# Half batch 4 of the attention turned by the DMA crossbar instead of by TensorE, with smaller masks and a new order of steps

## The chip, the cores and the metric

The kernel runs on one core of one Trainium2 chip. The metric is the device time in microseconds (us). Executions over 1.5% slower than the fastest of the same kernel are left out of the means. A ratio is the mean time of one kernel's fast runs over that of the other's of the same rounds, so it is not quite the ratio of the medians that stand beside it. Brackets give its 95% interval.

## The reference

Windowed attention on 8 batches, 8 heads, 576 tokens, 64 dimensions, and then a two-layer feed-forward over all 4608 tokens:

```python
rel = pos[:, None] - pos[None, :]
mask_plain = (rel >= 0) & (rel < 32)                              # heads 0 to 3
mask_dil = (rel >= 0) & (rel < 32 * 4) & (rel % 4 == 0)           # heads 4 to 7
scores = np.where(masks, q @ k.T / sqrt(64), -1e9)
attn = exp(scores - max) / sum                                    # over the keys
x = (attn @ v) rearranged to (4608 tokens, 512)
h = x @ w_in                                                      # 512 -> 2048
out = np.maximum(0.01 * h, h) @ w_out                             # 2048 -> 512
```

## The kernel before

The kernel is a list of steps, given as one string and issued in that order; each engine works off its own share in order. PE is TensorE, DVE VectorE, ACT ScalarE, POOL GpSimd and SP SyncE. A half batch n is four heads of one batch (even n the plain heads, odd n the dilated ones), and it has three units of attention. The steps that the argument needs:

- `gq:n` and `lq:n` load q and k of a half batch, `gq` as f16 through POOL's (software) queue, `lq` as f32 on SP's queue. `lq:n:b:P` waits until POOL reaches it. `lv` loads v and `lw` the weights, both on POOL's queue.
- `cq`, `cv` cast or copy on V (DVE), P (POOL) or A (ACT).
- `B:n:pair:..` turns q and k on PE (2 x 18 transposes a call); `T:n` turns them by the DMA crossbar, the transpose that the DMA engines do on the way.
- `S`, `M`, `D` are scores, mask, values of a unit. `S:u:b` adds the mask as a bias by two matmuls on PE, `S:u:m` leaves it to `M` on DVE. `D:u:l` divides by a logarithm and an exponential on ACT, `D:u:r` by DVE's reciprocal.
- `I:c:j` and `O:t:g` are the two layers of the feed-forward.
- `Z:n` is n matmuls of zeros into a PSUM tile that nobody reads. They keep PE busy while data is still on its way; they are called warmers here.

```python
PROGRAM = """
Z:12 gq:3:b lq:1:1 lq:1:0 Z:1 cq:1:k:V:1 lv:1:b lq:0:0 lq:0:1 Z:2 bias cq:1:q:A:1 B:1:1:AA Z:2
... (some 600 steps more) ...
"""
NPE = 5                      # half batches below this are turned on PE

        elif f == "Z":
            wp = psa.tile([128, 512], FP32, tag="den", name="wp")      # one buffer
            for _ in range(int(a[0])):
                nc.tensor.matmul(wp, warm[:, 0:128], warm, start=True, stop=True)

    def transpose(n):                                                  # T:n
        ...
                nc.sync.dma_start_transpose(t.rearrange("p (c r) -> p c r", r=96), qkh[n, nm][0:96, 0:1536])

    def pe_transpose(n, p, nm, eng):                                   # B:n:p
        ...
                nc.tensor.transpose(tp[r, 64 * t:64 * t + 64], h[r, t, :], ident[r, r])

    def load_qk(n, pairs, gate=None):                                  # lq
        ...
            if gate is not None and nm == "q":
                gate.memset(t[0:1, 0, 0:1], 0.0)       # the load waits for this engine

    def ff_out(t, g, queue):
        if g == 0:
            ops[t] = psm.tile([128, 512], FP32, tag="pm", name="op")
        op = ops[t]
        ...
        for c0, c1 in ((0, 256), (256, 512)) if last else ((0, 512),):
            for j in range(0 if last else 4 * g, 4 * g + 4):
                nc.tensor.matmul(op[:, c0:c1], gt[:, j, g0:g0 + 128], w2[j // 4][:, j % 4, c0:c1], ...)
            if g == 3:
                nc.scalar.copy(out=ob[:, c0:c1], in_=op[:, c0:c1])
                queue.dma_start(out[128 * t:128 * t + 128, c0:c1], ob[:, c0:c1])
```

The softmax here doesn't subtract the row's maximum and nothing guards it: scores larger than these inputs give would overflow.

## Time and profile before

| | before |
|---|---|
| time | 322.21 us, 2 runs, 321.96 to 322.46; the profiled run took 321.16 |
| span of the profile | 319.5 us |
| PE busy | 98%, full clock in every slice |
| first feed-forward group starts | 26.51 us |
| last matmul starts | 315.93 us |

The profiled run is 1 us faster than the median of the same kernel. In the eleven runs of this kernel beside the first batch of experiments the times went from 321.17 to 323.33, so a difference of 1 us between two single traces says little.

PE's list of waits tells what is to be won at most: it lists for each line of the kernel what PE stood for, as total us, number of times, longest. L418 is the warmers, L359 the first layer and L374 the second.

```profile
PE wp L418 <- DVE xT L113: 1.3, 1, 1.3
PE hp L359 <- ACT gt L361: 1.0, 2, 0.6
PE op L374 <- ACT ob L378: 0.5, 1, 0.5
```

After the first warmer (which waits for its zeros) the waits come to about 2 us in all. A change can therefore take little more than what it takes from PE's own work.

The first feed-forward group, in the timeline of PE (start, duration, line, operation; a bracket at the end of such a line gives the idle time before it and what ended it):

```profile
26.51 1.49 PE L359 MATMUL hp<-xT,w 128*128 128x384 f16 x8
```

This is the view of PE's weight loads, one of which goes ahead of each matmul; the first column is its start, the second its duration:

```profile
3.45 0.15 PEld L418 LDWEIGHTS <-xT 128*128 128x128 f16 x1 [0.28 <-issue]
3.88 0.15 PEld L418 LDWEIGHTS <-xT 128*128 128x128 f16 x1 [0.28 <-issue]
4.31 0.99 PEld L418 LDWEIGHTS <-xT 128*128 128x128 f16 x5 [0.28 <-issue]
```

Inside a block the warmers follow each other every 0.43 us at first (3.45, 3.88, 4.31) and then every 0.215 us (five in 0.99): PE's clock starts at half, and the trace's record of the granted clock has the full one from 4.35 us on.

### The profile page before, as it was taken

How to read it: one execution, taken by the hardware profiler on the slowest of the kernel's cores; microseconds unless marked ns; L12 is line 12 of the kernel's file. 1: busy time of each engine (PE TensorE's matmuls, PEld its weight loads, DVE VectorE, ACT ScalarE, POOL GpSimd, SP SyncE). 2: the span in 40 equal slices, each digit the busy share in tenths (PEclk: the TensorE clock that was granted, in tenths of full speed). 3: DMA queues.
4: the chain of work that ended last, by engine and by line, in shares of the span. 5: the costliest groups of instructions: out<-in, count | busy, mean ns of one | idle time of the engine just before them, and what ended most of it. 6: DMA issues, size and time to landing. Idle time of an engine off the chain costs nothing.

```text
span 319.5 us, 6740 instructions
## 1 busy us (share of the span) xinstructions
PE 312.5 (98%) x2821; PEld 184.5 (58%) x2821; DVE 125.5 (39%) x196; ACT 190.8 (60%) x375; POOL 75.5 (24%) x113
## 2 busy tenths in 40 slices
PE   8999999999999999999999999999999999999995
PEld 3556765566655655665556556555665555655544
DVE  3586435354475675572521860423224340300000
ACT  3378872768666655767557926764774764453421
POOL 8683400253234043330041500430000000000001
PEclk9999999999999999999999999999999999999999
DMA  7999999999999829999399387391000000000102
GB/s 202 249 206 208 211 170 188 229 184 195 119 238 206 200 55 161 287 159 224 65 230 130 72 207 155 49 168 65 1 35 33 35 35 34 33 35 33 66 35 99
DMA packets 89902, 42.38 MB, mean 133 GB/s; under 512 B 69776, under 2 KB 85136, under 8 KB 89872
## 3 DMA queue, kind: packets, MB, share of 16 engines
q1 hardware_dynamic: 58080, 21.83, 34.7%
q0 software_dynamic: 29344, 15.93, 33.7%
q10 hardware_dynamic: 2448, 4.20, 3.6%
q8 instruction: 22, 0.36, 0.5%
q14 instruction: 8, 0.07, 0.1%
HBM read 36.70 MB, written 9.44 MB: 144 GB/s over the span
## 4 chain that ended last, share of the span: by engine, by line
PE 90%; ACT 4%; DMA 3%; issue 1%; POOL 0%; DVE 0%; ACTq 0%; POOLq 0%
PE hp L359 39%; PE op L374 38%; PE sps L286 4%; PE den L312 3%; DMA kh<-in_k_dram 3%; PE o L320 2%; ACT ln L325 1%; PE tp L233 1%; ACT rec L326 1%; PE wp L418 1%; ACT er L289 1%; PE sps L270 0%; ACT ob L378 0%; ACT gt L361 0%; POOL qh L169 0%
## 5 line engine op out<-in xcount | busy, mean ns | idle before, releaser
L359 PE MATMUL hp<-xT,w 128*128 128x384 f16 (+1 forms) x832 | 140.7, 314 | 1.3 <-ACT gt L361 1.0
L374 PE MATMUL op<-w,gt 128*128 128x512 f16 (+1 forms) x592 | 138.9, 374 | 0.5 <-ACT ob L378 0.5
L361 ACT ACTIVATE gt<-hp 128x384 f16<-128x384 f32 (+1 forms) x208 | 94.5, 465 | 65.9 <-PE hp L359 64.9
L359 PEld LDWEIGHTS <-w 128*128 128x128 f16 x832 | 89.6, 114 | 45.7 <-issue 2.5
L374 PEld LDWEIGHTS <-gt 128*128 128x128 f16 x592 | 56.0, 98 | 54.4 <-issue 0.6
L337 DVE TENSOR_TENSOR xT<-o,rec 128x384 f16<-128x384 f32 (+1 forms) x64 | 34.0, 554 | 81.0 <-ACT rec L326 75.9
L379 POOL DMA_DIRECT2D out_dram<-ob x20 | 11.3, 564 | 180.3 <-ACT ob L378 178.7
L328 DVE RECIPROCAL rec<-den 128x384 f32<-128x384 f32 x14 | 35.8, 2555 | 44.3 <-PE den L312 44.3
L289 ACT ACTIVATE er<-sps 128x768 f16<-128x768 f32 (+1 forms) x48 | 38.6, 804 | 20.8 <-PE sps L286 20.7
L378 ACT COPY ob<-op 128x512 f32<-128x512 f32 (+1 forms) x37 | 21.2, 573 | 28.3 <-PE op L374 28.2
L296 DVE TENSOR_TENSOR em<-er,mask 128x768 f16<-128x768 f16 (+1 forms) x43 | 26.8, 645 | 10.2 <-ACT er L289 10.0
L286 PE MATMUL sps<-qT,kT 64*128 64x96 f16 (+1 forms) x448 | 19.0, 209 | 0.1
L325 ACT ACTIVATE ln<-den 128x384 f32<-128x384 f32 x34 | 16.4, 483 | 3.8 <-PE den L312 3.3
L326 ACT ACTIVATE rec<-ln 128x384 f32<-128x384 f32 x34 | 17.8, 524 | 1.1
L286 PEld LDWEIGHTS <-kT 64*128 64x128 f16 (+1 forms) x448 | 12.1, 106 | 10.0 <-issue 7.1
L320 PEld LDWEIGHTS <-vh 128*64 128x64 f16 (+1 forms) x448 | 15.4, 110 | 2.4
L320 PE MATMUL o<-em,vh 128*64 128x96 f16 (+1 forms) x400 | 15.0, 201 | 0.0
L312 PE MATMUL den<-em,ones 128*64 128x384 f16 (+1 forms) x86 | 15.0, 345 | 0.0
L192 POOL CAST kh<-kf 96x512 f16<-96x512 f32 (+1 forms) x12 | 7.0, 627 | 31.7 <-DMA kf<-in_k_dram 31.7
L418 PE MATMUL wp<-xT 128*128 128x512 f16 x35 | 11.7, 431 | 1.7 <-DVE xT L113 1.3
L177 POOL DMA_DIRECT2D vh<-in_v_dram x8 | 10.7, 1339 | 5.1 <-PE hp L359 2.3
L182 POOL DMA_DIRECT2D vh<-in_v_dram x16 | 10.1, 637 | 2.5 <-PE o L320 2.2
(58 smaller groups left out, 114.3 us busy)
## 6 DMA issues: line engine op xcount, KB each, us to landing
out_dram<-ob POOLq DMA_DIRECT2D x20, 256.0 KB, 2.3
out_dram<-ob ACTq DMA_DIRECT2D x15, 256.0 KB, 2.0
qf<-in_q_dram SPq DMA_DIRECT2D x5, 576.0 KB, 7.0
kf<-in_k_dram SPq DMA_DIRECT2D x5, 576.0 KB, 7.8
vh<-in_v_dram POOLq DMA_DIRECT2D x8, 288.0 KB, 7.6
qf<-in_q_dram SPq DMA_DIRECT2D x6, 384.0 KB, 6.6
kf<-in_k_dram SPq DMA_DIRECT2D x6, 384.0 KB, 8.1
w<-in_moe_w_in_dram POOLq DMA_DIRECT2D x4, 512.0 KB, 12.0
```

The costliest lines, as they stand in the source:

```text
L286: nc.tensor.matmul(sps[0:kp, hh, w * x:w * x + w], ka, qa, start=not pe_mask, stop=not pe_mask or x == len(tiles) - 1)
L289: nc.scalar.activation(out=er[0:kp], in_=sps[0:kp, :, 0:384], func=AF.Exp, scale=SCALE)
L296: nc.vector.tensor_tensor(out=em[0:kp].rearrange("p h (t c) -> p h t c", c=w), in0=er[0:kp].rearrange("p h (t c) -> p h t c", c=w), in1=ba ...
L312: nc.tensor.matmul(den[64 * hh:64 * hh + 64, 0:384], ones[0:kp], em[0:kp, hh, :], start=True, stop=True)
L320: nc.tensor.matmul(o[64 * hh:64 * hh + 64, w * x:w * x + w], vt[0:kp, sl, :], em[0:kp, hh, w * x:w * x + w], start=True, stop=True)
L326: nc.scalar.activation(out=rec, in_=ln, func=AF.Exp, scale=-1.0)
L328: nc.vector.reciprocal(out=rec, in_=den[:, 0:384])
L337: nc.vector.tensor_tensor(out=out_x, in0=ins[0], in1=ins[1], op=ALU.mult)
L359: nc.tensor.matmul(hp[:, 0:w], w1[j // 4][:, i, j % 4::4], xT[:, i, x0:x0 + w], start=(i == 0), stop=(i == 3))
L361: nc.scalar.activation(out=gt[:, j, g0:g0 + w], in_=hp[:, 0:w], func=AF.Prelu, alpha=0.01)
L374: nc.tensor.matmul(op[:, c0:c1], gt[:, j, g0:g0 + 128], w2[j // 4][:, j % 4, c0:c1], start=(j == 0), stop=(j == 15))
L378: nc.scalar.copy(out=ob[:, c0:c1], in_=op[:, c0:c1])
```

## The change

The intent: PE is the bound, so two of its ten transpose calls go to the DMA crossbar; the last output tile gets a second PSUM tile so that its second half need not wait for a copy; the masks are built from 96 columns instead of 384 on POOL; and the whole order is redone.

```diff
-Z:12 gq:3:b lq:1:1 lq:1:0 Z:1 cq:1:k:V:1 lv:1:b lq:0:0 lq:0:1 Z:2 bias cq:1:q:A:1 B:1:1:AA Z:2
-cq:1:q:P:0 Z:4 lv:0:b Z:1 cq:1:k:V:0 Z:1 S:4:b gq:2:b B:1:0:AV ...
+Z:2 gq:3:b lq:1:1 lq:1:0 Z:1 lv:1:b lq:0:0 lq:0:1 Z:1 cq:1:q:P:1 bias Z:3 gq:2:b Z:1 lv:0:b lw:0:0
+mask Z:2 cq:1:k:V:1 Z:1 cq:1:q:A:0 Z:9 B:1:1:VA cq:1:k:V:0 Z:7 lw:0:1 lw:0:2 Z:2 S:4:b B:1:0:AV ...
+... lw:1:1 I:0:1 D:2:lp lq:4:b:P I:0:2 I:0:3 M:11 lq:5:b:P ... cv:3:P:b I:0:13 I:0:14 cq:4:k:P:b
+D:9:rp I:0:15 I:1:0 Z:2 D:11:r ... cq:4:q:P:b I:1:4 O:0:0 B:2:0:AA I:1:5 M:10 lv:2:b lv:4:b lv:5:b
+... cq:5:q:A:b O:2:0 cv:2:P:b ... T:5 T:4 lq:6:b ... Z:1 M:8 D:7:lp ...
@@
-    NPE = 5
+    NPE = 4
@@ masks
-    def band(t, one, other):         # POOL: two memsets, two selects, 384 columns, for bias and for mask
+    def band_bias():                 # POOL: two selects of 96 columns; DVE copies them three times
+    def band_mask():
+        nc.vector.tensor_scalar(out=mask, in0=bias, scalar1=-1.0, scalar2=None, op0=ALU.is_ge)
@@ ff_out
         for c0, c1 in ((0, 256), (256, 512)) if last else ((0, 512),):
+            if c0:
+                op = psm.tile([128, 512], FP32, tag="pm", name="op")
```

(The program string is cut; the memset of `ident` also moves from POOL to DVE.) The first 15 warmers of before stand in three blocks ahead of the first transposes (12, 1 and 2).

## The prediction

> **What bounds the kernel now.** I read the page first (busy times, then the slices), then the chain of waits in order of time, then the timelines of the first 50 us and the last 15, and last the DMA queues stretch by stretch.
>
> ```profile
> PE 312.5 (98%) x2821; PEld 184.5 (58%) x2821; DVE 125.5 (39%) x196; ACT 190.8 (60%) x375; POOL 75.5 (24%) x113
> PEclk9999999999999999999999999999999999999999
> PE 90%; ACT 4%; DMA 3%; issue 1%; POOL 0%; DVE 0%; ACTq 0%; POOLq 0%
> ```
>
> PE is busy for 98% of the span, at full clock, and is 90% of the chain that ended last; no other engine passes 60%. The matmul ends are modelled, so I check it by rate. In the chain in order of time, groups that run without a wait read like this:
>
> ```profile
> 184.01 1.30 PE hp L359 x8
> 185.31 1.73 PE op L374 x8
> 314.30 1.92 PE op L374 x16
> ```
>
> That is 162 ns for a 384-wide matmul of the first layer, 216 ns for a 512-wide one of the second, 120 ns for the 256-wide ones of the end; a run of twelve 192-wide ones takes 0.99 us, 82 ns each. So the feed-forward alone is 704 x 0.162 + 128 x 0.082 + 560 x 0.216 + 32 x 0.120 = 114.0 + 10.5 + 121.0 + 3.8 = 249 us of PE. Attention (48 score steps at 0.28 to 0.46, 48 value steps at 0.45) adds some 36 us, the PE transposes 10 x 0.69 = 7, the warming matmuls about 9. Sum 301 of 319.5. What is left is start, end, some waits in the first 30 us, and about 0.1 us at each of some tens of changes of work. Once the feed-forward has begun, PE hardly waits: the chain leaves PE for a few us at three places only (56 to 60, 174 to 179, 253 to 256 us), mostly overlapped; lost there is 0.4 to 0.7 us each.
>
> Two edges matter. The lead-in: the first feed-forward group starts at 26.5 us, a second burst at 28.6. And the end:
>
> ```profile
> 313.88 0.37 ACT L378 COPY ob<-op 128x256 f32<-128x256 f32 x1 [1.16 <-PE op L374]
> 314.28 0.34 ACTq L379 DMA_DIRECT2D out_dram<-ob  x1
> 314.30 1.91 PE L374 MATMUL op<-w,gt 128*128 128x256 f16 x16 [0.46 <-ACT ob L378]
> ```
>
> Here PE stands 0.46 us because both halves of the last token tile share one PSUM tile, and the second waits for the copy of the first.
>
> The third thing to see is the DMA. The slices show it 99% busy up to about 100 us. In the stretch 33 to 38 us its queues read:
>
> ```profile
> q0 software_dynamic: 268, 0.98, 96.7%
> q1 hardware_dynamic: 266, 0.07, 10.0%
> ```
>
> Equal packets, but the weights (software queue) move 3.7 KB in each and the half batch load on the other queue 256 B. A half batch of the even kind, loaded while weights flow, crawls. The load of half batch 6, issued at 29.5 us, landed 17.5 (q) and 26.5 us (k) later.
>
> **What the Trainium skill says.** "VectorE: DVE Perf Modes", The three transpose paths: 390 ns for a 128x128 transpose on TensorE, 1309 ns by the DMA crossbar. In this trace 36 transposes of 64x64 keep PE for 0.69 us, and one crossbar instruction holds its queue 1.2 to 4 us and lands after 5 to 6: slower, but not on PE. The trade is only good because PE is the bound. "TensorE: Matmul & The Clock Gate", Back-to-back issue gap: N/2.4 + 2.5 ns, 216 for N = 512; the trace has 216. So no order makes the feed-forward cheaper. "DMA: Bandwidth & Descriptors", Issuing engines are not separate DMA queues: all queues share the 16 engines and interleave; the equal packets above agree.
>
> **The change part by part.**
> 1. Half batch 4 leaves PE: two calls, 72 transposes, 2 x 0.69 = 1.4 us off PE, all in the stretch where PE is the bound (67 to 71 us). Gone too are three ACT copies (0.64 each) and one on DVE (0.75), which do not bound. In their place come an f32 load, two casts on POOL of 1.6 us each and two crossbar transposes on SP.
> 2. End: a PSUM tile of its own for the last half, -0.46 us.
> 3. Biased scores: 7 instead of 5 steps are masked on PE, two matmuls of 384 columns each (0.33 us a step). One is in the lead-in (counted in 5), one later: +0.33 us. Two mask multiplications (0.64) leave DVE.
> 4. Division by logarithm in 37 steps instead of 34: DVE loses 3 x 2.55 us, ACT gains 3 x 1.0. Neither is the bound.
> 5. Masks and lead-in. POOL loses two 384-wide memsets and four 384-wide selects of 0.5 to 0.6 us (now two of 96 columns), some 2.5 us; DVE gains about 0.6. But POOL's early work is feeding DMA queues that have a backlog until 43 us, so this does not bring data 2.5 us sooner. The fixed points stay: k of half batch 3 lands at 12.1 us and the software queue delivers in its order. I walked the new order by hand from 12.5 us, when the transposes of 3:0 are done, with the durations of this trace. The last cast for 0:1 (POOL, after data at 14.8) is ready at 16.2; 0:1 turned to 16.9; value step 3 to 17.4, seven warmers to 18.9, step 4 to 19.4, scores 0 to 20.1, three warmers, transposes 3:1 to 21.4, scores 1 to 22.1, transposes 2:1 to 23.2, step 1 to 23.7, scores 11 to 24.4, steps 0 and 5 to 25.8, scores 2 to 26.5. ACT, which takes more of the copies now, is full from 19.4 and gives step 0 its reciprocal at 26.5, so the product is there at 27.3 and the first feed-forward group starts then. Five groups, value step 2 and scores 9 are done at 31.4. The old kernel has these at 32.0 and besides them scores 7 and 10 and the transposes 2:0 (0.3 + 0.3 + 0.69 = 1.3 us). So the new lead-in is 31.4 + 1.3 - 32.0 = 0.7 us behind. There are 50 warming matmuls for 35; the 12 more before the first group (12 x 0.215 = 2.6 us) fill time that would be waited.
> Sum of what is sure: -1.4 - 0.46 + 0.33 + 0.7 = -0.8 us.
> 6. The DMA order. Loads of half batches 4 and 5 are now issued behind the second-layer weights' first two requests. The old trace fits a rule of eight software transfers in flight (the ninth stands until the first lands), so POOL reaches the gate of these loads at about 20.5 us, not 29.5. They contend with weights. I estimate their landing from the old trace: there q of half batch 5 landed at 58.9, behind all that the new one has ahead of it plus the v of 2, 5 and the q, k of 4, which used about 8.3 us of the DMA between 42 and 57. So q of 5 lands at about 50.6, k of 4 a little before. ACT, which now casts q of 5 itself, is reached at about 49. POOL casts 4 to about 52, issues v of 2 behind that, and it lands 7.6 us (median row) after 51.9, at 59.5; the copy of 1.5 us makes 61, while PE wants it at about 58. This may cost 0 to 4 us; whoever wrote the order placed one warmer just there, so a short wait was seen. I take +0.6.
>
> **The rivals.**
> A. PE work falls and nothing else happens: -1.4 - 0.46 + 0.33 is -1.5, and if the lead-in gains from earlier requests (weights asked for at 8 to 13 us instead of 13 to 16) 1 to 2 us more: 318.5 to 320.5. For it: PE's 90% of the chain. Against: the DMA backlog.
> B. A load wait takes the place of the PE work: ACT stands on q of 5 and PE on v of 2 at 48 to 62 us: 324 to 328. For it: 256 B packets crawl behind weights, and POOL stood 23.0 us on k of half batch 5 in the old trace, with v requests now behind such a wait. Against: the old order met its landings nearly exactly, so the new one was likely fitted with care.
> C. ACT becomes the bound in the lead-in, through copies moved from DVE: +1 to +2 us, 322 to 324. Over the whole it has 40% to spare.
>
> **Range and chances.** Before is 322.2. -0.8 + 0.6, and some weight on A because such an order is usually kept when it helps, gives 321.4. Eight in ten: 317.5 to 326. To be 2% faster (under 315.8) PE would have to lose 6.4 us; removed work, end and all found waits together hardly reach that: 4%. To be 2% slower (over 328.7) needs B in full: 5%. Within 2%: 91%.
>
> **What would show it.** PE rows: the transposes at 288 instead of 360, the bias matmul at 14, warmers 50. The last half starting without a wait on ACT. First feed-forward group at 27 to 28 us; if at 24 or 25, my lead-in is wrong and A is right. Feed-forward rates unchanged at 162 and 216 ns. Around 48 to 62 us: PE busy throughout speaks for A; an idle PE released by DVE or ACT, behind POOL's copy of v 2 or the cast of q 5, speaks for B. Two more crossbar rows than 34. Wrong altogether if the clock falls, or if transposes in the DMA hold back later loads so that score steps after 90 us wait.

## The result, and the profile after

325.79 us (two runs, 325.23 and 326.35) against 322.21: ratio 1.0111 [1.0075, 1.0146]. The time is within 2% of before and inside the predicted range, if only by 0.2 us. But the prediction's own estimate lay 0.8 us below the old kernel, and the time came out 3.6 us above.

The page of after: busy times, then the chain that ended last by engine and by line.

```profile
PE 317.0 (98%) x2768; PEld 184.0 (57%) x2768; DVE 105.6 (33%) x172; ACT 201.7 (62%) x396; POOL 76.6 (24%) x112
...
PE 85%; DMA 11%; POOL 1%; ACT 1%; issue 1%; DVE 1%; POOLq 0%
PE op L382 35%; PE hp L365 35%; DMA kf<-in_k_dram 8%; PE wp L426 4%; PE sps L292 4%; PE den L318 3%; DMA vh<-in_v_dram 2%; PE o L326 2%; PE tp L239 1%; PE sps L276 1%; POOL qh L207 0%; POOL vh L216 0%; ACT rec L332 0%; POOL kh L207 0%; DVE xT L343 0%
```

Two things stand out. PE issues 53 matmuls fewer (2768 for 2821: 72 transposes gone, 15 warmers and 4 bias matmuls more), and yet it is *busier*, 317.0 for 312.5 us. And the chain now goes over DMA for 11% of the span; the load of k alone (`kf`) is 8%. The list of PE's waits (L326 is the product with v):

```profile
PE wp L426 <- DVE xT L119: 1.4, 1, 1.4
PE o L326 <- POOL vh L216: 1.3, 1, 1.3
PE hp L365 <- DVE xT L343: 0.4, 1, 0.4
```

The waits on ACT are gone, one on POOL's copy of v has come. The waits after the first warmer are hardly longer than before (2.2 us for 1.9), so most of the 5 us of span stands in the trace as busy time of PE, not as waits.

Where in time? The first feed-forward group starts 3.1 us later, in the timeline of PE:

```profile
29.57 1.46 PE L365 MATMUL hp<-xT,w 128*128 128x384 f16 x8 [0.44 <-DVE xT L343]
```

and the last matmul starts at 320.98 for 315.93, 5.05 us later. I added up PE's start-to-start times (from the start of one matmul to the start of the next), split at the start of the 21st matmul of the first layer, where five groups are done:

| part | us | how |
|---|---|---|
| lead-in, to that matmul | +3.2 | 33.95 - 31.98, and 1.25 of attention work (scores 7 and 10, transposes 2:0) that after has still to do there |
| 72 transposes off PE | -1.37 | their start-to-start time |
| last output tile | -0.62 | the wait of 0.46 and the restart behind it |
| bias matmuls | +0.42 | one more biased score step after this point |
| wait for v of half batch 2 | +1.5 | 1.67 start-to-start, where 0.19 is usual |
| three late warmers (`Z:2`, `Z:1`) | +1.0 | their time and the restarts around them (but see e10) |
| rest | +0.9 | not itemized; PE changes its kind of work 309 times for 296 in this part |
| sum | +5.0 | |

Since before's trace is 1 us faster than its median and after's 0.6 slower, some 1.6 of the 5.0 is chance between two runs; the medians differ by 3.6.

**The lead-in.** The warmers in it take 14.48 us of PE's start-to-start time for 11.20 before: +3.28, about as much as the lead-in lost. Part of that is number, part is how they are cut up. The view of the weight loads, after:

```profile
2.50 0.10 PEld L426 LDWEIGHTS <-xT 128*128 128x128 f16 x1 [0.54 <-issue]
3.14 0.10 PEld L426 LDWEIGHTS <-xT 128*128 128x128 f16 x1 [0.54 <-issue]
3.78 0.10 PEld L426 LDWEIGHTS <-xT 128*128 128x128 f16 x1 [0.54 <-issue]
...
7.14 1.61 PEld L426 LDWEIGHTS <-xT 128*128 128x128 f16 x8 [0.34 <-issue]
```

The first three stand at the head of new blocks and come 0.64 us apart, not 0.43: a new block is a new tile in the one buffer, and its first matmul comes only about when the last one of the block before has ended (the trace gives a warmer 379 ns in the median and 634 at most, so the spacing of 0.64 is one whole matmul, where inside a block the next one follows into the one under way). It costs 0.21 us a block here. The full clock was granted at 6.24 us for 4.35. At full clock a new block costs as much (0.43 us start to start for 0.215). The row of warmers before the first transposes tells the sum (start, duration, count), before:

```profile
1.35 5.31 PE L418 MATMUL wp<-xT 128*128 128x512 f16 x15 [1.35 <-DVE xT L113]
```

and after:

```profile
1.41 7.84 PE L426 MATMUL wp<-xT 128*128 128x512 f16 x20 [1.41 <-DVE xT L119]
```

**The load of half batches 4, 5 and v 2.** In the chain of waits in order of time (start, duration, what):

```profile
22.05 27.07 DMA kf<-in_k_dram
...
49.24 0.06 POOL kh L207
...
50.02 0.82 POOL kh L207
50.84 1.50 POOL qh L207 x2
52.33 7.75 DMA vh<-in_v_dram
...
60.13 1.41 POOL vh L216
```

k of half batch 4 is asked for at 22.05 and has landed after 27 us; only then does POOL cast it, cast q, issue v of half batch 2, wait 7.75 us for it, and copy it. PE came to this product at about 60.1 and ran it at 61.59:

```profile
61.59 0.36 PE L326 MATMUL o<-em,vh 128*64 128x96 f16 x8 [1.31 <-POOL vh L216]
```

Why 27 us: the DMA queues of after in the stretch 35 to 40 us (packets, MB, share of an engine):

```profile
q0 software_dynamic: 272, 0.97, 95.9%
q1 hardware_dynamic: 271, 0.07, 10.1%
```

The two queues move as many packets as each other, but the weights put 3.6 KB in one (0.97 MB over 272) and the half batch 256 B (0.07 MB over 271). The Trainium skill, "DMA: Bandwidth & Descriptors", Queues, rings and completion order, says that each engine goes round between its queue rows at packet granularity; this trace agrees, 272 to 271 (what the trace counts as a packet, of 256 B or 4 KB, may be smaller than the page's). A load in small packets gets a small share of the bytes (here 0.07 MB of 1.04) for as long as a queue of large packets is full.

**The end** is as planned. Before had a gap of 0.46 us between the two halves of the last tile; after the second-layer matmuls run in one row of 59 to the end, the change of tile within it:

```profile
311.76 9.48 PE L382 MATMUL op<-w,gt 128*128 128x512 f16 x59
```

### The profile page after: what moved, and what is told of

It reads as the page before. It is cut to its first block, busy times and chain, and to the rows that moved or that the text cites. A ratio compares the mean times of both kernels' runs of the same rounds, so it can differ in the third digit from the quotient of the medians.

```text
span 324.6 us, 6650 instructions
## 1 busy us (share of the span) xinstructions
PE 317.0 (98%) x2768; PEld 184.0 (57%) x2768; DVE 105.6 (33%) x172; ACT 201.7 (62%) x396; POOL 76.6 (24%) x112
## 3 DMA queue, kind: packets, MB, share of 16 engines
HBM read 36.70 MB, written 9.44 MB: 142 GB/s over the span
## 4 chain that ended last, share of the span: by engine, by line
PE 85%; DMA 11%; POOL 1%; ACT 1%; issue 1%; DVE 1%; POOLq 0%
PE op L382 35%; PE hp L365 35%; DMA kf<-in_k_dram 8%; PE wp L426 4%; PE sps L292 4%; PE den L318 3%; DMA vh<-in_v_dram 2%; PE o L326 2%; PE tp L239 1%; PE sps L276 1%; POOL qh L207 0%; POOL vh L216 0%; ACT rec L332 0%; POOL kh L207 0%; DVE xT L343 0%
## 5 line engine op out<-in xcount | busy, mean ns | idle before, releaser
L365 PE MATMUL hp<-xT,w 128*128 128x384 f16 (+1 forms) x832 | 142.4, 315 | 0.4 <-DVE xT L343 0.4
L295 ACT ACTIVATE er<-sps 128x768 f16<-128x768 f32 (+1 forms) x48 | 38.6, 804 | 14.2 <-PE sps L292 12.2
L387 POOL DMA_DIRECT2D out_dram<-ob x17 | 9.5, 558 | 144.3 <-ACT ob L386 144.0
L334 DVE RECIPROCAL rec<-den 128x384 f32<-128x384 f32 x11 | 28.1, 2555 | 30.8 <-PE den L318 30.8
L302 DVE TENSOR_TENSOR em<-er,mask 128x768 f16<-128x768 f16 (+1 forms) x41 | 24.7, 622 | 19.0 <-ACT er L295 18.8
L331 ACT ACTIVATE ln<-den 128x384 f32<-128x384 f32 x37 | 18.0, 487 | 6.0 <-PE den L318 5.5
L332 ACT ACTIVATE rec<-ln 128x384 f32<-128x384 f32 x37 | 19.4, 524 | 1.2
L292 PEld LDWEIGHTS <-kT 64*128 64x128 f16 (+1 forms) x448 | 12.0, 106 | 13.1 <-issue 11.7
L326 PEld LDWEIGHTS <-vh 128*64 128x64 f16 (+1 forms) x448 | 15.6, 110 | 3.8 <-POOL vh L216 1.6
L426 PE MATMUL wp<-xT 128*128 128x512 f16 x50 | 15.6, 419 | 1.9 <-DVE xT L119 1.4
L326 PE MATMUL o<-em,vh 128*64 128x96 f16 (+1 forms) x384 | 14.4, 201 | 1.3 <-POOL vh L216 1.3
L183 POOL DMA_DIRECT2D vh<-in_v_dram x8 | 9.8, 1223 | 17.4 <-issue 17.4
L198 POOL CAST kh<-kf 96x512 f16<-96x512 f32 (+1 forms) x20 | 11.5, 619 | 1.5 <-DMA kf<-in_k_dram 1.4
L318 PEld LDWEIGHTS <-ones 128*64 128x64 f16 (+1 forms) x96 | 5.5, 107 | 10.0 <-issue 7.6
```

Source lines behind the costliest of these rows:

```text
L292: nc.tensor.matmul(sps[0:kp, hh, w * x:w * x + w], ka, qa, start=not pe_mask, stop=not pe_mask or x == len(tiles) - 1)
L295: nc.scalar.activation(out=er[0:kp], in_=sps[0:kp, :, 0:384], func=AF.Exp, scale=SCALE)
L302: nc.vector.tensor_tensor(out=em[0:kp].rearrange("p h (t c) -> p h t c", c=w), in0=er[0:kp].rearrange("p h (t c) -> p h t c", c=w), in1=ba ...
L318: nc.tensor.matmul(den[64 * hh:64 * hh + 64, 0:384], ones[0:kp], em[0:kp, hh, :], start=True, stop=True)
L326: nc.tensor.matmul(o[64 * hh:64 * hh + 64, w * x:w * x + w], vt[0:kp, sl, :], em[0:kp, hh, w * x:w * x + w], start=True, stop=True)
L334: nc.vector.reciprocal(out=rec, in_=den[:, 0:384])
```

## The experiments

Two theories at the outset. **Warmers**: the lead-in is late because its warmers cost PE time, by number and by cutting. **Loads**: the early demand for the half batches 4 and 5 makes a deadline near 61 us, whatever happens before it. The rivals: chance (one trace, a late clock grant), and contention in the DMA that merely moves if v goes first. All results in one table (medians of the fast runs); "first group" and "last matmul" are starts in the trace, "clock" is when the full clock was granted in it. The median of the runs of before in the four batches was 322.49 (a0, e1, e2, e6), 322.19 (e4, e8, e5, e9), 322.20 (e7, e10, e12) and 322.51 (e13).

| run | median us | ratio to before | first group | last matmul | clock |
|---|---|---|---|---|---|
| before, first trace | 322.21 | | 26.51 | 315.93 | 4.35 |
| after, first trace | 325.79 | 1.0111 [1.0075, 1.0146] | 29.57 | 320.98 | 6.24 |
| a0_same | 326.11 | 1.0118 [1.0091, 1.0146] | 29.57 | 320.11 | 6.62 |
| e1_one_block | 325.24 | 1.0077 [1.0055, 1.0100] | 28.49 | 320.61 | 5.37 |
| e2_twelve | 325.57 | 1.0101 [1.0071, 1.0131] | 28.24 | 320.18 | 5.25 |
| e6_before_split | 323.61 | 1.0032 [1.0016, 1.0049] | 29.53 | 318.55 | 7.13 |
| e4_v2_early | 326.96 | 1.0147 [1.0129, 1.0164] | 29.56 | 321.85 | 6.48 |
| e8_lead_v2 | 327.41 | 1.0161 [1.0143, 1.0179] | 28.88 | 322.45 | 6.22 |
| e5_all | 328.30 | 1.0172 [1.0145, 1.0198] | 28.11 | 323.31 | 6.42 |
| e9_pe4 | 326.95 | 1.0138 [1.0118, 1.0159] | 29.81 | 321.83 | 7.02 |
| e7_end_masks | 321.84 | 0.9982 [0.9965, 0.9999] | 28.72 | 316.81 | 6.81 |
| e10_pe4_lead | 324.62 | 1.0079 [1.0065, 1.0093] | 27.65 | 319.52 | 5.82 |
| e12_order_kept | 321.56 | 0.9987 [0.9970, 1.0003] | 27.97 | 316.11 | 4.77 |
| e13_order_moved | 321.20 | 0.9963 [0.9945, 0.9980] | 27.25 | 315.61 | 5.50 |

### a0_same: the changed kernel again

No edit.

> The changed kernel unaltered, as a control on this chip. Two theories of the 5.0 us by which its last matmul came later in the traces. Warmers: 47 warming matmuls instead of 35 before the first feed-forward group, cut into many small blocks, each on a new PSUM tile that waits for the block before; they keep PE from the real work and the full clock is granted later (6.2 us after the start for 4.4). Landings: the lead-in is held by the data, and warmers only fill waits. Both expect here 325 to 326.5, ratio 1.010 to 1.013, first transposes at about 9.2 us. If the late clock was chance, this trace may have it at 4 to 5 us and the first transposes at 8 or sooner.

326.11, ratio 1.0118: the loss is real, on another set of runs. First group at 29.57 again, clock at 6.62. But PE does not wait for v 2 here: POOL had k of 4 half a us earlier, v 2 landed in 6 us instead of 7.75, its copy was done at 59.23, and PE came at 60.12 (61.59 with the wait in the first trace):

```profile
60.12 0.34 PE L326 MATMUL o<-em,vh 128*64 128x96 f16 x8
```

Of the 1.5 us, 0.6 are lost again before and at the next product (63.49, the list names DVE), and the last matmul started 0.87 us sooner than in the first trace. So the lead-in repeats, and the wait on v 2 comes and goes, between 0 and 1.5 us. (The 0.4 us on v 2 that later expectations give for this trace is a misreading: that is the delay at the product after it.)

### e1_one_block: after, its first 20 warmers in one block

```diff
-Z:2 gq:3:b ... Z:1 lv:1:b ... Z:1 cq:1:q:P:1 bias Z:3 gq:2:b Z:1 ... Z:2 cq:1:k:V:1 Z:1 cq:1:q:A:0 Z:9 B:1:1:VA
+Z:20 gq:3:b ... lv:1:b ... cq:1:q:P:1 bias gq:2:b ... cq:1:k:V:1 cq:1:q:A:0 B:1:1:VA
```

> The changed kernel with its 20 warming matmuls ahead of the first transposes in one block at the start, not in eight. Warmers theory: no tile changes, spacing 0.43 us at half clock, clock granted near 4.4 us, 20 matmuls done at 7.2 instead of 9.2; the lead-in ends about 1.5 to 2 us sooner, about 324.0. Landings theory: the first transposes move up but the first feed-forward group stays within 0.5 us of 29.6, time 325.5.

The row of warmers in PE's timeline is 1.4 us shorter than after's (7.84 above) for the same 20:

```profile
1.41 6.42 PE L426 MATMUL wp<-xT 128*128 128x512 f16 x20 [1.41 <-DVE xT L119]
```

and the first group starts 1.1 us sooner. The time fell by 0.9 (326.11 to 325.24; the intervals just overlap). In the trace the gain is not at the end: the wait on v 2 has grown.

```profile
PE o L326 <- POOL vh L216: 2.0, 1, 2.0
```

Warmers theory: right in kind. Loads theory: what the lead-in gives is partly taken at 61 us.

### e2_twelve: after, with 12 + 1 warmers instead of 20

```diff
-Z:2 gq:3:b ... (eight blocks, 20 in all) ... B:1:1:VA
+Z:12 gq:3:b ... Z:1 B:1:1:VA
```

> The changed kernel with 12 warming matmuls in one block and one more ahead of the first transposes, 13 instead of 20. Warmers theory: first transposes at 6.8 us, when the cast of k is ready, so 0.4 us sooner than with 20 in one block and 2.4 sooner than now; about 323.5. Landings theory: first feed-forward group within 0.5 us of 29.6, about 325.5; or slower if the clock falls back.

325.57, ratio 1.0101: hardly better than a0_same (the intervals overlap), although the first transposes start 2.9 us sooner (6.42 for 9.36) and the first group 1.3. The list of waits says where it went:

```profile
PE o L326 <- POOL vh L216: 1.8, 1, 1.8
PE tp L239 <- DMA kh<-in_k_dram: 1.7, 1, 1.7
```

Of 2.9 us, 1.7 are waited for k of half batch 3, still in the lead-in. At the product with v 2 PE then waits 1.8 and goes on at 60.80 (the same row of the timeline as shown above for after, where it is 61.59):

```profile
60.80 0.36 PE L326 MATMUL o<-em,vh 128*64 128x96 f16 x8 [1.85 <-POOL vh L216]
```

So there are two deadlines that loads set, near 13 and near 61 us, and at these places a warmer more or less is filler, just as the prediction said. Most of the gain in the lead-in is swallowed.

### e6_before_split: before, its first 13 warmers cut up like after's

```diff
-Z:12 gq:3:b lq:1:1 lq:1:0 Z:1 cq:1:k:V:1 ...
+Z:2 gq:3:b Z:1 Z:1 lq:1:1 lq:1:0 Z:3 Z:1 Z:2 Z:1 Z:1 Z:1 cq:1:k:V:1 ...     (13 still)
```

> The kernel before with its first 13 warming matmuls cut into nine blocks as small as the changed kernel's, the number unchanged. Warmers theory: each new block waits about 0.2 us for the one before, the clock is granted up to 2 us later, first transposes at 8 to 8.5 instead of 6.6 us, time +1 to +2, 323.2 to 324.2, ratio 1.003 to 1.006. Landings theory: 322.2, ratio within 0.001 of 1.

323.61 for 322.49, ratio 1.0032 [1.0016, 1.0049]: cutting alone, with nothing else of the change, costs 1.1 us. The rows of PE's timeline, to be held against before's 5.31 us and 6.59 for the start of the transposes:

```profile
1.34 7.54 PE L418 MATMUL wp<-xT 128*128 128x512 f16 x15 [1.34 <-DVE xT L113]
8.82 0.47 PE L233 MATMUL tp<-ident,qh 64*64 64x64 f16 x18
```

The same 15 (ten blocks for three) take 2.2 us longer in this trace. Seven extra blocks at 0.21 us are 1.5 of them; the rest goes with the clock, granted at 7.13 here. Whether cutting delays the grant is not settled: in five traces with cut blocks it came at 6.24, 6.48, 6.62, 7.02 and 7.13, in nine with the first warmers in one block between 4.35 and 6.81. Later on average (6.7 for 5.6), but the sets overlap. There is a grid in it: in all fourteen traces each stretch at full clock that ends within the trace lasts a whole multiple of 3.413 us (314.03, 317.44 and 320.85 us are 92, 93 and 94 times that). Where this grid lies against the kernel's start differs from run to run, so part of the grant's time is chance.

### e4_v2_early: after, v of half batch 2 asked for before the casts of 4

```diff
-... cv:3:P:b I:0:13 I:0:14 cq:4:k:P:b ... M:10 lv:2:b lv:4:b lv:5:b ...
+... cv:3:P:b lv:2:b I:0:13 I:0:14 cq:4:k:P:b ... M:10 lv:4:b lv:5:b ...
```

> The changed kernel with the request for v of half batch 2 moved ahead of the casts of k and q of half batch 4 on POOL, which wait for the load of 4 (49 us). In its traces PE stands 0.4 to 1.6 us at 60 to 63 us on the copy of v 2, and the software queue moves 6 packets from 45 to 50 us. Load theory: the wait vanishes, the last matmul comes 0.4 to 1.6 us sooner, 324.5 to 325.5, ratio 1.007 to 1.009. Rival, contention: 2304 packets of v now slow the load of 4 and 5, ACT and DVE stand on their casts, and the wait moves there: no gain or a loss, 326 to 327.

326.96, ratio 1.0147; slower than after's 1.0111 and 1.0118 if anything. The wait on v 2 is gone from the list, but the loads of 4 and 5 came later for it. Timeline of POOL, ACT and PE:

```profile
52.60 1.59 POOL L207 CAST kh<-kf 96x768 f16<-96x768 f32 x2 [18.93 <-DMA kf<-in_k_dram]
```

```profile
54.62 2.18 ACT L198 CAST qh<-qf 96x512 f16<-96x512 f32 x4 [2.38 <-DMA qf<-in_q_dram]
```

```profile
57.77 0.49 PE L365 MATMUL hp<-xT,w 128*128 128x192 f16 x4 [1.57 <-ACT gt L367]
```

The cast of k 4 starts at 52.60 for 49.24, ACT stands 2.38 us for q of 5 and starts its casts at 54.62 for 52.16, and PE stands 1.57 us for ACT, which is behind with the activations. The wait has moved from POOL to ACT. That is the contention rival: v of 2 is now asked for at 32.47, while k of 4 (asked for at 22.71) is still on its way, and makes it late. The queues of e4 from 45 to 50 us have both at work: q0 moves 0.22 MB of v, and q1's packets take 85.0% of the engines' time for 0.72 MB. In after q1 has that stretch nearly to itself (q0 0.02 MB) and needs 55.9% for 0.71.

### e8_lead_v2 and e5_all: both cures at once

e8 is e2 and e4 together; e5 also drops the three late warmers.

```diff
-I:1:0 Z:2 D:11:r ... Z:1 M:8 D:7:lp
+I:1:0 D:11:r ... M:8 D:7:lp
```

> The same with 13 warming matmuls in one block at the start instead of 20 in eight. Alone that brought the first feed-forward group 1.3 us sooner and the end nothing, as the wait for v 2 grew from 0.4 to 2.1 us. Load theory: with v 2 early both gains reach the end, 1.3 + 0.4 to 1.6 us off 326.1: about 323.5, ratio 1.003 to 1.004. Rival: another load (4 or 5) holds the same point, and the time stays above 325.

> The same and without the three warming matmuls after the feed-forward has begun (0.96 us of PE in the traces, waits for the block before included). Two of them stood before value step 11, one before the wait for v 2. Load theory: PE is the bound there again, so up to 0.9 us more: about 322.7, ratio 1.000 to 1.002. If they only filled waits: as the run without this edit, 323.5.

327.41 and 328.30: worse than e2 alone and no better than e4 (e8's interval overlaps e4's). In e8 the sooner PE comes, the longer it stands for ACT:

```profile
PE hp L365 <- ACT gt L367: 2.9, 1, 2.9
```

and in e5 for 3.0 us. In e5's trace the granted clock then falls to half for 3.4 us (57.6 to 61.0), behind that wait and with the late warmers gone; in e8's it does not. The mean granted clocks of the runs point the same way, as such a stretch costs 0.005 of the mean: 0.989 to 0.995 in all five runs of e5, 0.999 to 1.000 in e4's four. But e8 has two runs at 0.993 and 0.995 and before five of eleven at 0.995 in the first batch, so this is a hint of what the late warmers may be for and no more. As a cure for after's loss both fail.

### e9_pe4: after, but half batch 4 back on PE

```diff
-    NPE = 4
+    NPE = 5
-... lq:4:b:P ... cv:3:P:b ... cq:4:k:P:b ... cq:4:q:P:b ... lv:2:b lv:4:b lv:5:b ... T:5 T:4 ... S:17:m ... S:12:m
+... cv:3:P:b ... lv:2:b gq:4:b lv:4:b lv:5:b ... T:5 ... S:17:m B:4:0:AV ... B:4:1:AA S:12:m
```

> The changed kernel with half batch 4 back on PE: its f16 load on the software queue behind v 2, no casts of 4, no crossbar transposes of 4, 72 PE transposes in their old place before its scores. So v 2 is early here too. If the crossbar in itself saves its 1.4 us of PE, this is 1.4 slower than the run with v 2 early alone: 326 to 327. If the load of 4 on the other queue is what costs (256 B packets, casts that block POOL), it is as fast or faster than the changed kernel: 324 to 326.

326.95, ratio 1.0138. No load wait is on PE's list any more: without the gated load of 4 the rest lands in time. But the 1.4 us of transposes are back on PE, and together it is no better than after (1.0111, 1.0118; the intervals overlap). So moving half batch 4 to the crossbar is not what makes the new order slow. Something that e9 shares with after does.

### e10_pe4_lead: e9 with 12 + 1 leading warmers and no late ones

```diff
-Z:2 gq:3:b ... (eight blocks, 20 in all) ... I:1:0 Z:2 D:11:r ... Z:1 M:8 D:7:lp
+Z:12 gq:3:b ... Z:1 B:1:1:VA ...             I:1:0 D:11:r ... M:8 D:7:lp
```

> The changed kernel with half batch 4 back on PE (whose trace had no wait on a load), 13 warming matmuls at the start in one block and none after the feed-forward has begun. There no load held PE, so if warmers cost time wherever no load takes the gain back, this gains 1.3 (lead-in) + 0.9 (late warmers): 326.95 less 2.2, about 324.7, ratio 1.007 to 1.009. If the loads of 5 to 7 or v hold PE also here, ratio 1.012 or more and a wait of 1 us or more in PE's list at 50 to 65 us.

324.62, ratio 1.0079 [1.0065, 1.0093], apart from e9's interval: -2.3 us. The first group starts at 27.65, 2.2 sooner than in e9, and the last matmul at 319.52, 2.3 sooner: where no load binds after the lead-in, all that the lead-in gives arrives at the end.
The late warmers give nothing: from the 21st first-layer matmul to the last, e9 takes 287.65 us and e10 287.49. Without them PE waits at two more places for DVE (three waits of 0.4 at most, 1.0 in all, on e10's list), so these three did fill time.

```profile
27.65 1.46 PE L365 MATMUL hp<-xT,w 128*128 128x384 f16 x8 [0.44 <-DVE xT L343]
```

Its list of waits has one for k of half batch 3:

```profile
PE tp L239 <- DMA kh<-in_k_dram: 0.7, 1, 0.7
```

(The expectation speaks of one block; the edit is that of e2, 12 and 1.) Seven warmers fewer ahead of the transposes, and the other 13 in two blocks, let these start 2.75 us sooner (6.69 for 9.44); 0.7 of that PE now waits for k of half batch 3, and 2.2 reach the first group. So only a part of the 20 filled time that PE would have waited. How large a part hangs on when k 3 lands. Up to the first group e2, e8, e5 and e10 have the same steps, and so have after, a0, e4 and e9 with the 20: the first groups of the one set start at 28.24, 28.88, 28.11 and 27.65, with waits for k 3 of 1.7, 1.9, 1.0 and 0.7 us; those of the other at 29.57, 29.57, 29.56 and 29.81, with none. That is 1.4 us on average, and e10's 2.2 is the lucky end. Most of it seems to be the cutting: e1's one trace, with the 20 in one block, has 28.49.

e10 also shows what is left: it is 2.4 us above before, with no wait of over 0.7 us on its list after the first warmer.

### e7_end_masks: before with the end tile and the small masks

```diff
+            if c0:
+                op = psm.tile([128, 512], FP32, tag="pm", name="op")
... and band_bias(), band_mask() of the change
```

> The kernel before, its order untouched, with two parts of the change alone: the PSUM tile of its own for the last half, and the small mask building. Prediction's terms: -0.46 us at the end, nothing from the masks: 321.7, ratio 0.9980 to 0.9990; in the trace the last sixteen matmuls start without the 0.46 us wait on ACT, first feed-forward group at 26.5 us give or take 0.3. Rival: the shorter mask work on POOL lets requests go sooner and the lead-in shrinks by 1 us or more: ratio below 0.996. Other rival: DVE's part of the mask building, which waits for POOL, holds the first cast of k (it did so to 6.7 us in the changed kernel): first transposes after 6.6 us, slower.

321.84, ratio 0.9982 [0.9965, 0.9999]: the end tile pays about what its wait was (0.36 us in the medians). The masks brought nothing that the trace shows: the first transposes came at 7.72 and the first group at 28.72, with the clock at 6.81, both later than in before's trace. The two parts were not tested apart, so a small loss by the masks is not excluded.

### e12_order_kept: before's order, half batch 4 on the crossbar, loaded later

Here half batch 4 takes the place of 6 in the load order, its units come behind those of 5, and the loads of 6 and 7 go behind the crossbar's work. Before's warmers stay.

```diff
-    NPE = 5
+    NPE = 4
-... lq:6:b:P ... gq:4:b ... cq:5:k:P:b ... cq:5:q:V:b ... cq:6:q:P:b ... T:5 lq:7:b B:4:0:AV cq:6:k:V:b ... B:4:1:AA S:12:m ...
+... lq:4:b:P ... cq:4:q:P:b cq:5:k:P:b ... cq:5:q:V:b cq:4:k:V:b ... T:5 T:4 lq:6:b lq:7:b ... S:15:m ... cq:6:q:P:b ... T:6 ...
 (units 12 to 14 and 15 to 17 change places; casts and T of 6 and 7 later; end tile as in the change)
```

> The kernel before with half batch 4 turned by the crossbar and the tile of its own at the end, and its order kept but for what this needs: 4 is loaded in the place of 6, half batch 5 is scored ahead of 4, the loads of 6 and 7 follow the crossbar transposes of 5 and 4. Lead-in and warmers untouched. If the crossbar's saving is real once no load is wanted too soon: -1.4 - 0.5 us, about 320.3, ratio 0.993 to 0.995. If the crossbar transposes or the loads moved behind them come too late for the scores of 5, 4 or 6 at 70 to 95 us, PE waits there and the ratio is 1.000 or more.

321.56, ratio 0.9987 [0.9970, 1.0003]. So the crossbar for half batch 4 does not lose in itself. It does not win clearly either: one wait has come in the place of the transposes, at 90.9 us, for the crossbar's transposes of half batch 6, which is loaded later here. The list of waits:

```profile
PE sps L286 <- DMA kT<-kh: 1.2, 1, 1.2
```

### e13_order_moved: e12 with two score steps of half batch 6 later

```diff
-O:6:1 S:20:m D:13:r ... D:12:lp S:18:m M:14 ... cq:9:k:P:b I:4:0
+O:6:1 D:13:r ... D:12:lp S:20:m M:14 ... cq:9:k:P:b S:18:m I:4:0
```

> The run before this one had all of PE's saving in its trace but one wait of 1.25 us on the crossbar transpose of half batch 6 at 90 us, whose load was moved behind those of 5 and 4. Here the two score steps of 6 are moved some 2 us later in the order, nothing else. If that wait was all that took the saving back, the wait is gone and the time falls by 1.2 to 1.4 us to about 320.2, ratio 0.993 to 0.996: a version that beats both kernels. If the delay just passes to a later point (7, or a chunk's first group), ratio 0.998 to 1.000.

321.20, ratio 0.9963 [0.9945, 0.9980] to before: faster than before (by 0.4%, at the edge of what this chip can tell) and than after. The wait at 90.9 is gone, but one of 0.7 us has come at 112.7, for the crossbar's transposes of half batch 9, so a part of the delay may have been passed on:

```profile
PE sps L286 <- DMA kT<-kh: 0.7, 1, 0.7
```

Against the end tile alone (e7, 0.9982) the crossbar's own share is -0.2%, and the intervals overlap. From the 21st first-layer matmul to the last, e13's trace takes 282.86 us, e7's 283.35 and before's 283.95: -0.5 for the crossbar, where the transposes alone are 1.4. It is a hint, not a proof.

## Why the prediction was right or wrong

Its direction was wrong: the steps it was sure of summed to -0.8 us, and +3.6 was measured. That the time fell inside its range (317.5 to 326) was partly luck: 325.79 is 0.2 us from the end, and the repeat's median is 326.11. By its own steps:

1. *Half batch 4 leaves PE, -1.4.* Right in the trace: 288 transposes, -1.37 us.
2. *End, -0.46.* Right: e7 shows 0.36 in the medians, the trace 0.62 with the restart.
3. *Biased scores, +0.33.* Right, if a little small: 14 bias matmuls, +0.42 start to start after the lead-in.
4. *Divisions, no effect on the bound.* Nothing speaks against it; DVE fell to 33%, ACT rose to 62%, and PE's list has no new wait on ACT in after.
5. *Lead-in, 0.7 us behind, the added warmers "fill time that would be waited".* **This is the step that failed.** In the trace the lead-in is 3.2 us behind; against the mean of the traces with before's lead-in uncut (before, e7, e12, e13: 32.75 us at the 21st matmul, where after has 33.95 and 1.25 us still to do) it is 2.45. The walk began at 12.5 us, when the transposes of 3:0 should be done; they were done at 14.2, so 1.7 of the 2.3 us by which the first group was missed (29.57 for 27.3) were lost before the walk's first step. It started behind the very place where the eight blocks of warmers stand, so it could not see them: it took the landing of k 3 at 12.1 us as the tie that would hold, and with 20 warmers in eight blocks PE was not there yet. k 3 landed at 12.64 in after, and PE never waited for it. It also priced the 12 added warmers at 0.215 us each, 2.6 in all, where the trace has 3.28: new blocks and the half clock are not in that price. With 12 + 1 warmers the tie does hold, as PE's waits for k 3 in e2, e8, e5 and e10 show. e6 (+1.1 for cutting alone) and these four traces (first group 1.4 us sooner on average, with seven fewer and fewer blocks) show what the warmers cost. The sentence on filler was right for the three late ones and for what PE then waits at k 3. In those four traces the lead-in comes to 32.60 + 1.25 = 33.85 on average, 1.1 behind the mean of before's, where 0.7 was forecast, so the rest of the walk was good.
6. *The DMA order, +0.6.* The mechanism, the order of events and the times were right: the gate of the loads was forecast at 20.5 and POOL reached it at 21.5, casts of 4 done at 52 (52.3), v 2 landed at 59.5 (60.1), copied at 61 (61.5). Its size in the first trace was 1.5, in the second 0; +0.6 was within that. The gate came out of the rule of eight software transfers in flight, and both traces fit it: up to 50 us POOL issues none while more than seven are on their way (in before it issues at 23.12, 25.62 and 28.16, each time 0.28 us after one of w_in has landed). PE came to the product at 60.1 and not at 58, because it was late by the lead-in: the failure of step 5 hid a part of step 6. In e1 and e2, which come sooner, this wait is 2.0 and 1.8. One reading was loose: the slices show the DMA at 90% or more up to about 100 us, which is not 99%.

Rival B was therefore true as a deadline rather than as a loss; its 324 to 328 held the result, but by a sum it did not name. Rival C (ACT in the lead-in) isn't seen in after. PE does wait for ACT at 57 us in e4, e8 and e5, but there a load holds ACT up. Rival A's view that early requests bring data sooner fell: the first weights were asked for at 8.04 us for 13.19 and landed at 24.49 for 22.84.

What stays open: e10 has neither after's waits nor its warmers and is still 1.0079. Its lead-in (32.03 + 1.25) is about 0.5 us behind before's mean. Of what comes later, 1.25 us is work moved out of the lead-in and thus counted already, 0.42 the bias matmuls;
and after the 21st matmul some 2.5 us more than in e7 remain (287.49 - 1.25 - 0.42 - 283.35). Added up by tile, 1.2 of them lie in the 192-wide matmuls of the first layer, mostly in two stops of 0.4 and 0.5 us near 42.7 and 60.2 us, where the late warmers were, and 0.7 in the 384-wide ones. PE changes its kind of work more often there (309 times for 296), and e10 has the short waits on DVE; neither was tested alone, so the new order's own cost is not explained in full. The prediction has no term for it: in the table of after it stands as the 1.0 of the late warmers and the 0.9 of the rest. Nor is the part that chance has in the clock grant.

## What to carry to other kernels

A filler matmul is free only while a load truly binds behind it: walk the engine's queue from the very first instruction, fillers included, and ask at each fill whether the data is there already; and put them in one block, since each new block on the same buffer waits for the one before (0.21 us a block here). Before moving a load earlier, look at the packet sizes of its neighbours in the queues: a load in 256 B packets beside weights in 3.6 KB ones ties down whatever engine is to cast it, and everything in that engine's order behind it. When a good change comes with a new order of everything, try it in the old order too: here that version (e13) came out 0.4% faster than before, and faster than after.

## What the Trainium skill lacked or had wrong

- "TensorE: Matmul & The Clock Gate", The HAM clock gate: it has the full clock about 4 us into sustained work, within 500 ns from run to run. The first matmul here starts at 1.34 to 1.41 us, and the grant came at 4.35 to 7.13 in fourteen traces, 3.0 to 5.8 us after it: a wider spread than that figure, though the section also says that the cold stretch differs from run to run. A spread of 4.35 to 6.81 is there even with the same leading block of warmers (before, e7).
- I found nothing on the same page that says what a new block of matmuls in a PSUM buffer that is written again costs: start to start 0.64 for 0.43 us at half clock, 0.43 for 0.215 at full.
- I found no page that weighs warming matmuls as work in an in-order queue: seven fewer at the start, and the rest in two blocks, were worth 1.4 us of lead-in on average over four traces each, 2.2 in e10.
- "VectorE: DVE Perf Modes", The three transpose paths: its 1309 ns are for one 128x128 block. The page has nothing on the crossbar beside other loads; here the crossbar instructions of the first 75 us (q or k of a half batch, or a part of it) took 2.7 to 8.4 us from issue to landing in before and 7.0 to 11.7 in after, and half batch 6 in e12 kept PE waiting 1.2 us.
- I found no page that says how long a load in small packets takes beside one in large packets: k of half batch 4 in 256 B packets beside weights took 27 us to land (22.05 to 49.1), and asking for v 2 while it was on its way delayed its cast by 3.4 us (49.24 to 52.60).
